# First K in three loads and four pieces, and job lists per PSUM bank in place of a list scheduler, in a fused attention and max-out kernel

## The chip, the cores and the metric

The kernel runs on one core of a Trainium2 chip. Its time is the device time of one execution in microseconds; lower is better. The core has a tensor engine (PE; its weight loads are listed as PEld), a vector engine (DVE), a scalar engine (ACT), GpSimd (POOL) and a sync engine (SP) whose queue issues nearly all DMAs. Sixteen DMA engines move the data.

## The reference

Queries are pooled by pairs of rows, attention is computed for 8 batches of 8 heads, and the result goes through a max-out layer:

```python
q_pool = q.reshape(B, H, S // 2, 2, D).mean(axis=3)      # B, H = 8, 8; S = 1152; D = 64
scores = np.matmul(q_pool, k.transpose(0, 1, 3, 2)) / np.sqrt(D)
attn = softmax(scores)                                    # over the keys
x = np.matmul(attn, v).transpose(0, 2, 1, 3).reshape(B * S // 2, H * D)
out = np.maximum(x @ w1, x @ w2) @ w_out                  # 4608 x 512, inner width 1024
```

All inputs and the output are float32. A guarded slow path (functions `guarded`, `softmax_head`, `softmax_rows`, `maxout`) is taken only where a sum of exponentials leaves a safe range; with these inputs it is not taken.

## The kernel before

**Tiling.** Two heads make a pair; there are 32 pairs. For each pair the kernel loads q, k and v (576 KB each), adds the two query rows of a pooling pair (`cast_q0` on DVE for the first two pairs, `cast_q` on POOL for the others), casts k to bf16 into `kbf` and transposes it into `kT` (nine tiles of 128 keys, called columns here; the first five pairs on PE with a DVE copy out of PSUM, `ktrans_pe`, the others by a transposing DMA). `scores(g)` then makes the scores of 512 (query, key) columns of both heads in a PSUM tile `sps`, and ACT takes their exponential into `et` (L745). Three such tiles are used in turn until group 33, two behind it. A pair is 10 1/8 groups. In pair 0 the queries come in two runs, so that groups 0 to 3 and half of group 4 need only the first 256 queries: group 0 needs key columns 0 and 1, group 1 columns 2 and 3, group 2 columns 4 and 5, group 3 columns 6 and 7.

**Behind the exponentials.** PE multiplies `et` with v (`av_jobs`, L649 and L661), DVE normalizes into `xnat`, which is transposed into `xT`. The max-out is computed as relu(x (w1 - w2)) w_out + x (w2 w_out): `wd` is w1 - w2 (POOL), `w21` is w2 times w_out (PE, L870), the hidden block is L925 or, for two PSUM banks at once, L952, and the output L985 or L1018. The weights are loaded between the first pairs' tensors and are cast by DVE reductions (L823, L827).

**The start.** The first K comes in two loads, columns 0-4 and 4-9, with the two halves of the first Q around them. ACT casts columns 0-2 and 2-4 (L519), POOL columns 4-9 (L522); PE transposes the three pieces and DVE copies them into `kT` (L625). Until real work is there PE runs groups of dummy matmuls on a constant tile (`fill`, L464, four of 128 columns; `short`, L473, eight of 64), which write a PSUM bank that nobody reads.

**What sets the order.** A `Plan` holds operations with the names that they read and write and derives the semaphore waits. `Plan.op` also keeps a model of the time of every engine. In the program's last part a list scheduler (`refill`, `options`, `choose`, `steady`, with a table of tuning values by time) uses that model to pick which job's next unit goes to PE. A job is a list of PE units and an evacuation; each of the eight PSUM banks ("0" to "7" in the strings) holds one job at a time. After that `Plan.reorder` puts the operations of PE, DVE, POOL and SP into the order of four written strings, in which a letter or digit names a lane (bank, load kind, "S" for a score group) and the dummy groups are letters of their own (U, V, y, z, Y, Z). ACT has no string: its order is that of creation.

**The names and lines that are spoken of.** `load_k` L484, `load_q` L494, `cast_k0` L519 and L522, `cast_k` L510, `cast_q0` L536, `cast_q` L543, `qtrans0` L585 and L592, `ktrans_pe` L618 and L625, `scores` L738 and L745, `w2t_job` L841 and L847, `h_jobs` relu on ACT L932, `p_job` copy on ACT L1045 and its last piece L1030 and L1034, `store` L889.

Of the kernel before, what the change touches and what calls it, by code (L numbers as in the profile page):

```python
# [9 lines left out]
P = 128  # L10
# [9 lines left out]
class Plan:  # L20

    INORDER = ("PE", "ACT", "DVE", "POOL")
    LAT = {"PE": 0.182, "ACT": 0.181, "DVE": 0.010, "POOL": 0.010}
    HEAR = {"PE": 0.046, "ACT": 0.024, "DVE": 0.024, "POOL": 0.075, "SP": 0.05}

    def __init__(self):
        self.ops = []
        self.writer = {}
        self.readers = {}
        self.free = {}  # L30
        self.dma_free = 0.0
        self.mode = None
        self.act_end = 0.0
        self.last = {}

    def deps(self, r, w, after=()):
        raw = {self.writer[k] for k in r if k in self.writer}
# [5 lines left out]
        return deps, raw  # L43

    def when(self, eng, r=(), w=(), after=(), fence=False):

        if any(k not in self.writer for k in r):
            return 1e9
        t = self.free.get(eng, 0.0)
        for d in self.deps(r, w, after)[0]:  # L50
            p = self.ops[d]
            if p["eng"] != eng or p["dma"] is not None or fence:
                t = max(t, p["seen"] + self.HEAR[eng])
        return t

    def op(self, eng, fn, r=(), w=(), dma=None, cost=0.1, mode="f", after=(), solo=False,
           fence=False):
        n = len(self.ops)
        assert all(k in self.writer for k in r), r
        deps, raw = self.deps(r, w, after)  # L60
        prev = self.last.get(eng)
        if prev is not None and (solo or self.ops[prev]["solo"]):
            deps.add(prev)
            raw.add(prev)
        self.last[eng] = n
        t = self.when(eng, r, w, after, fence)
        if dma is not None:
            if not self.dma_free:
                t = 0.78
            self.free[eng] = t + (1.3 if mode == "t" else 0.5)  # L70
            a = max(self.free[eng] + 1.2, self.dma_free)
            self.dma_free = a + cost + (0.9 if a < 5.0 <= a + cost else 0.0)
            seen = self.dma_free + 0.5
        else:
            if eng == "PE" and mode != self.mode:
                t = max(t, self.free.get("PE", 0.0) + 0.098)
                self.mode = mode
            busy = cost
            seen = t + cost + self.LAT[eng]
            if eng == "ACT":  # L80
                busy = cost + 0.051
                seen = max(seen, self.act_end + cost + 0.0735)
                self.act_end = seen
            elif eng == "DVE":
                busy = cost + 0.012
            self.free[eng] = t + busy
        self.ops.append(dict(eng=eng, fn=fn, deps=deps, raw=raw, dma=dma, w=tuple(w),
                             seen=seen, end=self.free[eng], solo=solo, fence=fence, r=tuple(r), at=n))
# [7 lines left out]
    def lane(self, o):  # L96
        key = (o["w"] or ("o",))[0]
        if o["eng"] == "PE":
            return "S" if key[0] == "s" else key[1:]
# [9 lines left out]
    def reorder(self, want):  # L109
# [5 lines left out]
        for eng, text in want.items():  # L115
            lanes = {}
            for n in line[eng]:
                lanes.setdefault(self.lane(ops[n]), []).append(n)
            assert sorted(c for c in text if c not in self.fill) == sorted(
                c for c, v in lanes.items() for _ in v)  # L120
            line[eng] = []
            for c in text:
                if c in self.fill:
                    m, mode, fn = self.fill[c]
                    key = f"f{m}"
                    nxt = ops[lanes[str(m)][0]]
                    n = len(ops)
                    ops.append(dict(
                        nxt, fn=fn, w=(key,), r=(), raw={self.writer["warm"]}, fence=False, at=n, inc=False, mode=mode, cost=0.0,
                        deps={d for d in nxt["deps"] if key in ops[d]["w"] and ops[d]["eng"] != eng}  # L130
                        | {self.writer["warm"]}))
                    nxt["deps"].add(n)
                    line[eng].append(n)
                else:
                    line[eng].append(lanes[c].pop(0))
# [75 lines left out]
class Job:  # L211


    def __init__(self, kind, units, evac, done=None, nb=None, single=None):
        self.kind, self.units, self.evac, self.done = kind, units, evac, done
        self.nb = nb
        self.single = single
# [137 lines left out]
def bass_funnel_attn__then__act_maxout2_kernel(  # L355
# [38 lines left out]
    with outer:  # L394
# [50 lines left out]
        def setup():  # L445
# [11 lines left out]
            op("DVE", lambda e: e.memset(xnat[0][:, 0, 0, :], 1.0), w=["warm"], cost=0.0)  # L457

        def fill(m, mode):
            z = slice(0, P) if mode == "f" else rows(0)  # L460
# [6 lines left out]
            return m, mode, go  # L467
# [85 lines left out]
        def unit(r, cost, go, mode="f"):  # L553

            def plan_it(m):
                op("PE", lambda e: go(e, m), r=r, w=[f"f{m}"], cost=cost, mode=mode)
# [1107 lines left out]
```

## Time and profile before

| what | us |
|---|---|
| median of 3 runs (364.25 to 365.19) | 365.12 |
| span of the profiled execution, first to last instruction | 363.3 |
| PE busy | 354.4 |
| ACT busy | 314.7 |
| DVE busy | 242.1 |
| POOL busy | 124.4 |

The profiled execution is listed by its span; the runs' time holds what lies around it as well. PE's busy time counts dummy matmuls, and matmuls are pipelined, so busy does not mean at peak. A group that ends the idle time of another engine is named behind an arrow. A DMA's time runs from its issue to its landing, queueing included.

### The profile page before, as it was taken

Reading aid. Unit: us, or ns where it says so; the run is one execution under the profiler, and the core shown is the slowest. Engines: PE = TensorE matmul, PEld = TensorE weight load, DVE = VectorE, ACT = ScalarE, POOL = GpSimd, SP = SyncE. Lnnn points to the kernel's source line nnn. Section 1 sums busy time; section 2 is a strip of 40 time slices with the busy share of each in tenths; the row PEclk is TensorE's granted clock in tenths of the full one; section 3 lists DMA queues with packets and bytes.
Section 4 is the critical chain, followed back from the end, with each engine's and each line's share of the span. In section 5 each row is a group of like instructions: output and inputs, shape, how many; then the busy total and the mean of one; then the engine's idle time right before and its main releaser. Section 6 shows DMA issues by size and latency. Waiting matters only on the chain.

```text
span 363.3 us, 13384 instructions
## 1 busy us (share of the span) xinstructions
PE 354.4 (98%) x5973; PEld 222.3 (61%) x5973; DVE 242.1 (67%) x526; ACT 314.7 (87%) x355; POOL 124.4 (34%) x111
## 2 busy tenths in 40 slices
PE   7998999999999999999999999999999999999995
PEld 6675655666564666657575665666666566656842
DVE  2777468877589777948968595676977847715421
ACT  4999999989999999999999999999999989894221
POOL 1246986344045433452251604613424320010000
PEclk9999999999999999999999999999999999999999
DMA  7999999999859998996999999986999570723106
GB/s 261 403 395 396 403 278 325 233 311 308 212 98 265 280 291 248 232 267 152 315 297 210 239 298 299 294 258 161 249 252 241 162 163 12 190 47 68 41 6 174
DMA packets 77790, 84.78 MB, mean 233 GB/s; under 512 B 50080, under 2 KB 50848, under 8 KB 77728
## 3 DMA queue, kind: packets, MB, share of 16 engines
q1 hardware_dynamic: 77168, 83.09, 85.8%
q8 instruction: 48, 0.79, 0.9%
q10 hardware_dynamic: 560, 0.79, 0.7%
q14 instruction: 14, 0.11, 0.1%
HBM read 62.91 MB, written 9.44 MB: 199 GB/s over the span
## 4 chain that ended last, share of the span: by engine, by line
PE 89%; ACT 7%; DMA 1%; issue 0%; SPq 0%; POOL 0%; DVE 0%; DVEq 0%
PE sps L738 20%; PE sps L649 13%; PE sps L985 11%; PE fb L985 10%; PE sps L952 9%; ACT et L745 7%; PE fb L649 7%; PE fb L952 7%; PE sps L1018 3%; PE sps L661 2%; PE fb L870 2%; PE fb L1018 1%; PE sps L925 1%; DMA kraw<-in_k_dram 1%; PE fb L661 1%; PE fb L925 1%
## 5 line engine op out<-in xcount | busy, mean ns | idle before, releaser
L745 ACT ACTIVATE et<-sps 128x1024 bf16<-128x1024 f32 (+1 forms) x336 | 306.7, 1006 | 19.7 <-PE sps L738 17.8
L738 PE MATMUL sps<-qpT,kT 64*128 64x256 bf16 (+7 forms) x1162 | 118.4, 283 | 0.7 <-ACT et L745 0.3
L603 DVE STREAM_TRANSPOSE qpT<-qp 32x288 bf16<-32x288 bf16 x216 | 101.4, 469 | 5.6 <-PE sps L738 1.5
L738 PEld LDWEIGHTS sps<-qpT,kT 64*128 64x128 bf16 x1162 | 47.9, 94 | 48.4 <-ACT et L745 16.3
L543 POOL TENSOR_TENSOR qp<-qraw 128x576 bf16<-128x576 f32 x30 | 42.1, 1405 | 89.6 <-DVE qpT L603 66.0
L549 POOL TENSOR_SCALAR vE<-vraw 128x1152 bf16<-128x1152 f32 x32 | 36.8, 1151 | 65.8 <-DMA vraw<-in_v_dram 63.4
L649 PE MATMUL sps<-vE,et 128*128 128x65 bf16 x1368 | 48.6, 193 | 0.4 <-issue 0.4
L649 PEld LDWEIGHTS sps<-vE,et 128*128 128x128 bf16 x1368 | 43.7, 97 | 6.5 <-issue 5.6
L510 POOL TENSOR_SCALAR kbf<-kraw 128x1152 bf16<-128x1152 f32 x31 | 35.6, 1151 | 33.4 <-DMA kT<-kbf 16.8
L952 PE MATMUL sps<-xT,wd 64*128 64x512 bf16 (+3 forms) x368 | 43.4, 326 | 0.0
L985 PE MATMUL sps<-wo,stage 64*128 64x512 bf16 x256 | 36.8, 376 | 0.0
L952 PE MATMUL fb<-xT,wd 64*128 64x512 bf16 (+3 forms) x272 | 33.5, 333 | 0.1
L649 PE MATMUL fb<-vE,et 128*128 128x65 bf16 x936 | 33.1, 193 | 0.0
L985 PE MATMUL fb<-wo,stage 64*128 64x512 bf16 x224 | 33.0, 376 | 0.0
L649 PEld LDWEIGHTS fb<-vE,et 128*128 128x128 bf16 x936 | 29.8, 97 | 4.8 <-issue 4.1
L961 DVE TENSOR_SCALAR stage<-sps 128x1024 bf16<-128x1024 f32 (+3 forms) x23 | 22.3, 969 | 15.4 <-PE sps L952 15.2
L961 DVE TENSOR_SCALAR stage<-fb 128x1024 bf16<-128x1024 f32 (+3 forms) x17 | 17.0, 999 | 10.7 <-PE fb L952 10.4
L952 PEld LDWEIGHTS sps<-xT,wd 64*128 64x128 bf16 x368 | 15.6, 94 | 13.5 <-PE sps L952 1.4
L671 DVE RECIPROCAL rcs<-sps 128x5 f32<-128x5 f32 (+1 forms) x38 | 7.0, 185 | 20.0 <-PE sps L649 19.5
L985 PE MATMUL sps<-w,xT 64*128 64x512 bf16 x128 | 18.8, 376 | 0.0
L996 DVE COPY stage<-sps 128x1024 f32<-128x1024 f32 x8 | 9.8, 1225 | 12.8 <-PE sps L985 12.7
L985 PEld LDWEIGHTS sps<-wo,stage 64*128 64x128 bf16 x256 | 12.1, 94 | 9.5
(88 smaller groups left out, 292.9 us busy)
## 6 DMA issues: line engine op xcount, KB each, us to landing
vraw<-in_v_dram SPq DMA_DIRECT2D x32, 576.0 KB, 6.6
kraw<-in_k_dram SPq DMA_DIRECT2D x31, 576.0 KB, 6.3
qraw<-in_q_dram SPq DMA_DIRECT2D x31, 576.0 KB, 6.1
out_dram<-stage SPq DMA_DIRECT2D x21, 256.0 KB, 5.8
out_dram<-stage SPq DMA_DIRECT2D x23, 128.0 KB, 3.3
xT<-in_moe_w_dram SPq DMA_DIRECT2D x4, 512.0 KB, 10.3
stage<-in_moe_w_out_dram SPq DMA_DIRECT2D x4, 512.0 KB, 14.0
stage<-in_moe_w_dram SPq DMA_DIRECT2D x4, 512.0 KB, 13.7
```

Of the source, the lines that this page charges most:

```text
L510: op("POOL", lambda g: g.tensor_scalar(kbf[s][:, :, :, :].rearrange("p t h d -> p h t d"), kraw[r][:, :, :, :], 1.0, 1.0, ALU.mult, ALU.mu ...
L543: op("POOL", lambda g: g.tensor_tensor(qpf[s][:, :, :], qraw[r][:, :, 0, :], qraw[r][:, :, 1, :], ALU.add), r=[f"qraw{r}"], w=[f"qp{s}.0", ...
L549: op("POOL", lambda g: g.tensor_scalar(vE[r][:, :, :, 0:D].rearrange("p t h d -> p h t d"), vraw[r][:, :, :, :], 1.0, 1.0, ALU.mult, ALU.m ...
L603: op("DVE", lambda e: e.transpose(view[dst:dst + 32, :, 32 * pb:32 * pb + 32], qpf[s][src:src + 32, :, 32 * db:32 * db + 32]), r=[f"qp{s}. ...
L649: last = e.matmul(fb[m][:, sb * 66:sb * 66 + 65], et[:, a:a + P], vE[vs][:, t, half, 0:65], start=(t == 0), stop=(t == NT - 1))
L661: last = e.matmul(fb[m][rows(half), NCH * 66:NCH * 66 + 65], et[:, a:a + NB], vE[vs][:, t, half, 0:65], start=(t == 0), stop=(t == NT - 1))
L738: last = e.matmul(sps[r][:, h, col:col + hi - lo], kT[i % 3][rows(h), t, :], qpT[i % 3][rows(h), lo:hi], start=True, stop=True)
L745: op("ACT", lambda e: e.activation(et2[:, :, c:c + z - a], sps[r][:, :, a - g * W:z - g * W], EXP, scale=scale), r=[f"s{r}"], w=keys + ([f ...
L952: last = e.matmul(fb[m + k][:, 0:size], wd[z, ct, (f0 + k) * P:(f0 + k + 1) * P], xT[z, ct, n0:n1], start=(turn == 0 and ct == 0), stop=(t ...
L961: dve(lambda e: e.tensor_scalar_max(gT[:, f0:f0 + 2, g0:g0 + size], wide[m // 2][:, :, 0:size], 0.0), [f"f{m}", f"f{m + 1}"], w + [f"f{m}" ...
L985: last = e.matmul(fb[m + k][:, :], lhs, rhs, start=(turn == 0 and j == 0), stop=(turn == 1 and j == NC_ + NF - 1))
L1018: return e.matmul(fb[m][:, 0:c1 - c0], lhs, rhs[:, c0:c1], start=(j == 0), stop=(j == NC_ + NF - 1))
```

## The change

There are two parts.

The loads and the pieces of the first K: three loads (columns 0-2, 2-6, 6-9), each with a semaphore of its own, and four pieces (0-2, 2-4, 4-6 on ACT, 6-9 on POOL), each cast, transposed by PE and copied by DVE. The first line of the PE string, the DVE string and the SP string change with it; the first score group goes alone ahead of the transposes of columns 2-6, and three groups of four dummy matmuls stand where five stood.

The schedule: the model of time, the scheduler and its tables go. In their place stands a list of jobs for each bank; one loop walks the PE string and creates each unit, each evacuation and, as soon as what they need has been created, the loads, casts and transposes. So PE's operations are created in their final order (the dummies too), while DVE, POOL and SP are still put into the order of their strings. ACT's order follows from the new order of creation.

```diff
-        K0 = (0, 2, 4, NT)
+        K0 = (0, 2, 4, 6, NT)
+        K0_LOADS = (0, 2, 6, NT)
...
-                    w=["kraw0.0"] if hi < NT else [f"kraw{s}"],
-                    dma="d_k" if hi < NT else f"d_k{s}", cost=0.0 if lo else 1.54)
+                    w=[f"kraw0.{lo}"] if hi < NT else [f"kraw{s}"],
+                    dma=f"d_k.{lo}" if hi < NT else f"d_k{s}")
...
             if hi < NT:
-                op("ACT", lambda e: e.activation(dst, src, COPY), r=["kraw0.0"], w=[f"kbf0.{lo}"],
-                   cost=(hi - lo) * 2 * D / 1200.0 + 0.03)
+                op("ACT", lambda e: e.activation(dst, src, COPY), r=[f"kraw0.{max(x for x in K0_LOADS if x <= lo)}"],
+                   w=[f"kbf0.{lo}"])
...
+        jobs_of = {
+            "0": "q0.0 k0.2 k0.6 q0.4 w1 q1.0 k1.5 w2 a0.1 k2.5 x0 a1.0 q3 k3.5 W0 W2 a4.0 H0.6 a6.0 "
...
+            "1": "k0.0 k0.4 k1.0 a0.0 q2 k2.0 w0 a1.1 w3 k3.0 x1 a4.1 a6.1 a8.1 a9.1 a10.1 a16.1 a17.1 "
...
         pe_order = (
-            "VVVVVVU0zz01SS0zzzSS0YSSYYSYYYS01SY0Sz0SSYSYY1S101S110SS000S1S01S01SSS000001S1S11SSS10SS101SS0S0"
+            "VVVVVVU01yS01SS0zzS0YSSYYSYYYS01SY0Sz0SSYSYY1S101S110SS000S1S01S01SSS000001S1S11SSS10SS101SS0S0"
...
+            later("lk0", [], lambda: load_k(0, tuple(zip(K0_LOADS, K0_LOADS[1:]))))
+            later("lq0", [], lambda: load_q(0, ((0, Q0[1]), (Q0[1], QU))))
+            later("cq0", ["lq0"], lambda: (cast_q0(0, 0, Q0[1]), cast_q0(0, Q0[1], QU)))
+            later("ck0", ["lk0"], lambda: [cast_k0(lo, hi) for lo, hi in zip(K0, K0[1:])])
...
+        for c in pe_order:
+            if c == "S":
+                scores(nxt)
+                nxt += 1
...
+            elif c in fills:
+                m, fn = fills[c]
+                op("PE", fn, r=["warm"], w=[f"f{m}"])
+            else:
+                m = int(c)
+                if c not in lane:
+                    name = left[c].pop(0)
+                    lane[c] = name, make(name)
+                name, job = lane[c]
+                job.units.pop(0)(m)
+                if not job.units:
...
+                    def end(c=c, m=m, job=job):
+                        job.evac(m)
+                        del lane[c]
...
+            settle()
...
         dve_order = (
-            "QQ0010Q0WQ0100WW0W1111001010W1W000W11010101W666666767TTT6T07T667T666TTTTTT60TTTTT006100T1T6TTTT6"
+            "QQ01010Q0WQ0100WW0W1111001010W1W000W11010101W666666767TTT6T07T667T666TTTTTT60TTTTT006100T1T6TTTT6"
...
         sp_order = (
-            "qkkqkwqvwwwqkwvwwwqkwwkvvqqqkwwvqtkqkvtkqktvkxxtvkqvtxxkxxqqkqqtvoxvxtvooxvxqtqkvqtokxokotkkxoov"
+            "qkkkqkwqvwwwqkwvwwwqkwwkvvqqqkwwvqtkqkvtkqktvkxxtvkqvtxxkxxqqkqqtvoxvxtvooxvxqtqkvqtokxokotkkxoov"
...
-        plan.reorder({"PE": pe_order, "DVE": dve_order, "POOL": pool_order, "SP": sp_order})
+        plan.reorder({"DVE": dve_order, "POOL": pool_order, "SP": sp_order})
```

`settle` runs everything that waits in `later`'s list for names that have been made; `make` turns a name of the lists into a job (`q` and `k` transposes, `a` attention times v, `x` transposes of the result, `w` and `W` weights, `h` and `H` hidden blocks, `p` and `P` outputs).

More of the change, by code (lines that the diff above doesn't have):

```diff
@@ L42, in deps @@
             deps.update(self.readers.get(k, ()))
[L43 to L88, printed above, removed]
+        self.ops.append(dict(eng=eng, fn=fn, deps=deps, raw=raw, dma=dma, r=tuple(r), w=tuple(w),
+                             fence=fence, at=n))
         for k in r:
@@ L118, in reorder @@
                 lanes.setdefault(self.lane(ops[n]), []).append(n)
[L119 to L135, printed above, removed]
+            assert sorted(text) == sorted(c for c, v in lanes.items() for _ in v)
+            line[eng] = [lanes[c].pop(0) for c in text]
         place = {}
```

774 lines of the change are left out of this document (187 added, 587 removed), and 14 rows, old and new, of the table jobs_of.

## The prediction

> **What bounds the kernel now.** I read the stages first (busy time of each engine per stretch), then the chain that ended last, then the timeline of the first 16 us, then the two places where data from memory meets that chain. The stages:
>
> ```profile
> core 0: us, PE busy (x) PEld busy (x) DVE busy (x) ACT busy (x) POOL busy (x), PEclk, DMA share, GB/s
> 3.75:4.75 1.00, 0.98 (x20) 0.79 (x18) 0.43 (x1) 0.20 (x1) 0.00 (x0) 1.00 0.93 306
> 5.50:7.25 1.75, 0.75 (x11) 0.28 (x10) 0.47 (x2) 0.99 (x2) 0.73 (x1) 1.00 0.96 342
> 17.25:30.00 12.75, 12.58 (x278) 8.97 (x276) 10.38 (x21) 12.75 (x16) 6.58 (x6) 1.00 1.04 396
> 30.00:34.00 4.00, 3.14 (x54) 2.07 (x56) 2.80 (x7) 4.00 (x5) 2.19 (x2) 1.00 1.05 391
> 36.00:41.00 5.00, 5.00 (x89) 2.79 (x86) 0.92 (x2) 4.87 (x6) 5.00 (x5) 1.00 1.03 407
> 41.00:359.66 318.66, 317.71 (x5305) 196.58 (x5301) 218.29 (x480) 278.59 (x315) 105.98 (x88) 1.00 0.87 217
> ```
>
> From 36 us to the last evacuation at 359.66 the tensor engine is busy 322.71 of 323.66 us: there the kernel is as long as its matmuls, and their order and number stay. So a change of the start is worth only what it moves the tensor engine's arrival at about 36 us. Until then the stages show a second limit: the DMA share is 0.93 to 1.05 from 4 us on, so loads land when the bytes in front of them are through, not when they are asked for.
>
> The chain that ended last, in order of time, over the first 45 us:
>
> ```profile
> 1.73 4.63 DMA kraw<-in_k_dram
> ...
> 6.44 0.74 POOL kbf L522
> 7.18 0.05 issue
> 7.22 0.45 PE fb L618 x5
> 7.68 0.67 PE fb L464 x12
> 8.35 0.34 PE sps L738 x4
> 8.69 0.02 issue
> 8.71 26.76 ACT et L745 x30
> ```
>
> Read alone it says: the second part of the first K lands at 1.73 + 4.63 = 6.36, is cast in one piece of 0.74, transposed, and then thirty exponentials run without a gap from 8.71 to 35.47 (0.89 each). Whoever gets the third exponential out before 8.71 would then win that time. The ScalarE's own rows (timeline: start, duration, line, what it writes and reads, count, idle before and who ended it) show a hole ahead of the third:
>
> ```profile
> 4.54 0.72 ACT L519 ACTIVATE kbf<-kraw 128x256 bf16<-128x256 f32 x2 [2.47 <-DMA kraw<-in_k_dram]
> 6.26 1.94 ACT L745 ACTIVATE et<-sps 128x1024 bf16<-128x1024 f32 x2 [1.00 <-PE sps L738]
> 8.71 1.02 ACT L745 ACTIVATE et<-sps 128x1024 bf16<-128x1024 f32 x1 [0.51 <-PE sps L738]
> ```
>
> Two exponentials, then 0.51 of waiting for the third group's scores, whose kT comes from the second load.
>
> **The change part by part.** Its first part is the loads. The first K arrives as columns 0-2, 2-6 and 6-9 in place of 0-4 and 4-9.
>
> ```profile
> 1.27 0.93 SPq L484 DMA_DIRECT2D kraw<-in_k_dram  x2
> 2.24 0.47 SPq L494 DMA_DIRECT2D qraw<-in_q_dram  x1
> ```
>
> ```profile
> kraw<-in_k_dram SPq DMA_DIRECT2D x1, 320.0 KB, 4.6
> qraw<-in_q_dram SPq DMA_DIRECT2D x1, 320.0 KB, 5.1
> qraw<-in_q_dram SPq DMA_DIRECT2D x1, 256.0 KB, 3.0
> kraw<-in_k_dram SPq DMA_DIRECT2D x1, 256.0 KB, 3.3
> ```
>
> The sync queue issues one DMA more, 0.47, ahead of the second half of Q and of everything behind it in that queue (the next K, the first weights, Q of pair 1, the first V). The Q half is issued at 2.24 and lands 5.1 later, so a later issue of 0.47 is hidden by the transfers in front of it; without that cover it would cost 0.47. Bytes stay equal, packets rise from 512 to 768 (each is one row's columns). The price of 256 more packets is not in the trace. Upper end: packets of 1 to 1.3 KB move 306 GB/s (3.75 to 4.75), those of 2.3 KB and more 396 GB/s (17.25 to 30); as a fixed time for each packet that is 1152/306 - 1.79 x 1.152 = 1.7 ns, with the slope (2304/396 - 1152/306)/1.152 = 1.79 ns a KB, and 256 of them make 0.44 us. [...] I take 0.1, nearer to nothing, since 3.75 to 4.75 still belongs to the start-up and its rate is low for other reasons too. [...]
>
> Landings: part one has half the bytes of today's first, 131 KB at 306 GB/s = 0.43 earlier than 4.54, so 4.11 to 4.54. Part two ends two columns into today's second load, which needs 6.36 - 4.54 = 1.82 for five columns: pro rata 5.27; by the rate 4.54 + 0.43 = 4.97; at the latest with today's second load, 6.36.
>
> The casts: the ScalarE casts columns 0-2, 2-4 and now 4-6, all three ahead of its first exponential, since its order is that of creation. So here is an added wait: exponential 0 now stands behind a cast that needs load two. Two casts take 0.72, so exponential 0 starts at 5.27 + 0.72 + 0.06 = 6.05 (from 5.75 to 7.14), today 6.26. GpSimd casts three columns in place of five, 0.44 for 0.74, and the four transposed pieces need one more VectorE copy; both engines idle there (DVE 0.47 busy in the 1.75 us from 5.50), cost nothing. On the tensor engine three groups of four dummy matmuls stand where five stood, and the first score group runs alone ahead of columns 2-6. If nothing waits, the hole of 0.51 is gone: exponentials back to back from 6.05, where the present run, counted back from 8.71 at 0.89 each, begins in effect at 6.93. The start gains 0.9 us (from 1.2 down to a loss of 0.2).
>
> **How much of it arrives.** Two places ahead of 36 us are clocked by memory and not by the ScalarE. First, pair 1. VectorE, TensorE and ScalarE rows:
>
> ```profile
> 10.47 1.22 DVE L823 TENSOR_REDUCE xT<-xT 128x1024 bf16<-128x1024 f32 x1 [0.94 <-DMA xT<-in_moe_w_dram]
> 11.96 0.76 DVE L536 TENSOR_TENSOR qp<-qraw 128x576 bf16<-128x576 f32 x1 [0.27 <-DMA qraw<-in_q_dram]
> ```
>
> ```profile
> 14.73 0.40 PE L618 MATMUL fb<-ident,kbf 128*128 128x128 bf16 x4
> 15.06 0.46 PE L738 MATMUL sps<-qpT,kT 64*128 64x64 bf16 x6
> ```
>
> ```profile
> 15.96 1.11 ACT L745 ACTIVATE et<-sps 128x1024 bf16<-128x1024 f32 x1
> 5.83 0.61 PE L738 MATMUL sps<-qpT,kT 64*128 64x256 bf16 x8 [0.22 <-DVE kT L625]
> ```
>
> The w2 cast and pair 1's Q both wait for their DMA; from them follow, in the fixed order of the VectorE and the tensor engine, the w2 and Q copies, the second half of K1 (14.73) and score group 10 (15.06), with no ScalarE wait between. An exponential follows its scores' start by 6.26 - 5.83 = 0.43, so exponential 10, now at 15.96, cannot start before 15.49: of 0.9 at most 0.47 is left. Second, pair 3:
>
> ```profile
> 17.56 1.00 SPq L484 DMA_DIRECT2D kraw<-in_k_dram  x1
> kraw<-in_k_dram SPq DMA_DIRECT2D x1, 576.0 KB, 13.4
> 29.64 1.41 POOL L543 TENSOR_TENSOR qp<-qraw 128x576 bf16<-128x576 f32 x1 [0.34 <-DMA qraw<-in_q_dram]
> 31.16 1.15 POOL L510 TENSOR_SCALAR kbf<-kraw 128x1152 bf16<-128x1152 f32 x1
> 32.45 0.22 PE L618 MATMUL fb<-ident,kbf 128*128 128x128 bf16 x1 [0.21 <-DVE qpT L576]
> ```
>
> K of pair 3 lands at 17.56 + 13.4 = 30.96, whatever the ScalarE did, because the DMA engines are full (1.04). GpSimd ends its cast at 32.31 and the tensor engine transposes it at 32.45. The wait named there is VectorE's, which follows the shifted stream; right behind it stands GpSimd, which does not. So at most 32.45 - 32.31 less a semaphore's 0.04 = 0.10 of the gain gets past 32.45; the rest becomes idle time of the tensor engine in 30 to 34, where it idles 0.86 already. From there everything is tensor work. A loss, in contrast, is not clipped: the VectorE wait would move on.
>
> The schedule's second part, job lists for the scheduler, leaves the tensor engine's order behind its first line as it was, and the VectorE and SP strings gain one letter each. The ScalarE's order is not written out and now follows the creation order: near the end two pairs change places.
>
> ```profile
> 352.01 0.38 ACT L932 ACTIVATE stage<-sps 128x256 bf16<-128x256 f32 x1 [5.17 <-PE sps L925]
> 352.30 0.58 ACT L1045 COPY stage<-sps 128x512 f32<-128x512 f32 x1
> ```
>
> The output copy (352.30) goes ahead of the last hidden block's relu (352.01). The ScalarE idled 5.17 before that, so the copy and its store run in that gap; the relu waits for its matmuls as now. Gain nothing to 0.1, cost nothing; if the copy came late the relu would, by at most the copy's 0.58.
>
> Sum: 0.10 gained at 32.45, 0.10 lost to packets (K3 lands later too), up to 0.1 at the end: -0.05 us on the span of 363.3. The median of the runs shown, 365.12, is 1.8 above that span, the part outside it, which stays. Forecast 365.0 us.
>
> **The rivals.** B, the whole start arrives: if VectorE latencies and not GpSimd hold pair 3, and pair 1's chain slides as well, 0.9 to 1.2 us come through: 364.2 to 363.9. For it: the unbroken run of thirty exponentials. Against it: the rows at 10.47, 11.96 and 31.16. C, slower, one mechanism: exponential 0 behind the third cast. If load two lands like today's second, at 6.36, exponential 0 starts at 7.14, 0.21 behind the effective 6.93, the scores of groups 1 and 2 stand behind the same cast, and with the packets' 0.44 it is 365.8. It passes 0.3% from a landing at 6.8 on with the packets' full price, at 7.25 without it (8.03 less 0.78). For it: today's second load is the slowest of the four by its bytes (4.6 for 320 KB right behind 3.3 for 256 KB). D, slower: with fewer dummies the tensor clock drops. Row 5.50 shows 0.75 busy of 1.75 at a granted 1.00, so holes of that size do not do it; if they did, these 0.75 and as much again would double: 365.9 to 366.6. [...] E, the change does nothing to the start because columns 2-6 come no sooner: 365.1.
>
> **How the numbers follow.** A measurement of this kernel can tell about 0.3%, 1.1 us; the runs shown lie 0.94 apart. Forecast A with E 0.66, all same; B 0.18, of it 0.14 faster beyond 1.1 with the scatter and 0.04 within; C 0.12, of it 0.06 slower; D 0.04 slower. That makes 0.14 faster, 0.76 same, 0.10 slower. The likeliest case alone spans 364.6 to 365.5; the range takes in most of B and C, 364.0 to 365.9.
>
> **What would show it.** Right: three casts on the ScalarE, exponential 0 at about 6.05, no hole before the third; score group 10 still near 15; K3's cast still ending near 32.3 and its transposes within 0.1 of 32.45; more tensor idle time in 30 to 34 than 0.86. Wrong: K3's transposes at 31.9 or earlier (B), exponential 0 beyond 6.9 (C), a granted clock below 1.00 before 16 us (D), or any new idle time behind 36 us, which would mean that the lists changed more than the start.

## The result and the profile after

The changed kernel takes 366.17 us in the median of 22 runs (364.68 to 370.39); the kernel before, beside it on the same chip, 364.99 (364.03 to 366.18, 22 runs). The ratio is 1.0041, 95% interval 1.0025 to 1.0058: slower, with an interval that leaves out 1, and above the forecast's range (364.0 to 365.9). The median lies 1.2 us above the predicted 365.0.

The ratios leave out executions more than 1.5% above the fastest of their kernel (one here), but the change alters how often an execution takes some 4 us more, so those above 367.9 us are counted below for every kernel (5 of the 22 here, none of the 22 of before).

The profiled execution has a span of 364.5 us, before 363.3. Stages of the changed kernel, columns as in the prediction (line numbers from here on are those of the changed kernel: L450 and L441 cast K on the ScalarE and on GpSimd, L467 adds Q's rows, L542 transposes K, L661 makes the scores, L668 their exponential):

```profile
3.75:4.75 1.00, 1.00 (x21) 0.84 (x18) 0.27 (x2) 0.42 (x1) 0.00 (x0) 1.00 0.67 135
5.50:7.25 1.75, 1.00 (x11) 0.38 (x12) 0.43 (x2) 1.23 (x3) 0.51 (x1) 1.00 1.01 356
...
12.00:17.25 5.25, 4.54 (x81) 3.01 (x79) 4.00 (x7) 5.11 (x6) 1.15 (x1) 1.00 1.04 407
17.25:30.00 12.75, 12.15 (x263) 8.86 (x261) 10.46 (x21) 12.48 (x15) 6.37 (x6) 1.00 1.04 396
30.00:34.00 4.00, 3.84 (x73) 2.45 (x69) 3.07 (x7) 3.90 (x6) 2.41 (x2) 1.00 1.05 392
36.00:41.00 5.00, 4.69 (x59) 1.98 (x57) 1.52 (x3) 4.87 (x6) 5.00 (x5) 1.00 1.03 406
41.00:359.66 318.66, 318.23 (x5337) 197.49 (x5336) 218.00 (x479) 279.47 (x315) 106.37 (x88) 1.00 0.89 217
```

Two things differ. Between 3.75 and 4.75 us the DMA engines move 135 GB/s where they moved 306. And in 30 to 34 the tensor engine, which idled 0.86 there, idles 0.16: its stream comes later, so the slack in front of pair 3 is gone. In 36 to 41 it idles 0.31 (before 0.00), behind 41 us 0.43 (before 0.95), together 0.74 where it was 0.95. All of the loss of this execution is made at the start. The ScalarE's rows of the timeline there:

```profile
3.93 0.42 ACT L450 ACTIVATE kbf<-kraw 128x256 bf16<-128x256 f32 x1 [1.86 <-DMA kraw<-in_k_dram]
6.02 0.72 ACT L450 ACTIVATE kbf<-kraw 128x256 bf16<-128x256 f32 x2 [1.67 <-DMA kraw<-in_k_dram]
6.65 3.80 ACT L668 ACTIVATE et<-sps 128x1024 bf16<-128x1024 f32 x4
10.79 2.85 ACT L668 ACTIVATE et<-sps 128x1024 bf16<-128x1024 f32 x3 [0.34 <-PE sps L661]
```

Three casts, the first exponential at 6.65, four in a row, and then a new hole of 0.34 at 10.79. Where that hole and the rest come from, the loads by issue (KB, us from issue to landing; the sync queue issues Q's halves at 0.79 and 2.75, the three K parts at 1.27, 1.73 and 2.24, the next K at 3.26):

```profile
kraw<-in_k_dram SPq DMA_DIRECT2D x1, 576.0 KB, 7.0
qraw<-in_q_dram SPq DMA_DIRECT2D x1, 320.0 KB, 6.0
...
kraw<-in_k_dram SPq DMA_DIRECT2D x1, 256.0 KB, 4.3
kraw<-in_k_dram SPq DMA_DIRECT2D x1, 192.0 KB, 4.4
kraw<-in_k_dram SPq DMA_DIRECT2D x1, 128.0 KB, 2.6
```

Part two lands at 1.73 + 4.3 = 6.0, Q's second half at 2.75 + 6.0 = 8.8 where it was 2.24 + 5.1 = 7.3, and the next K at 10.2 to 10.3. That K's row of before, issued at 2.75, puts its landing at 9.2:

```profile
kraw<-in_k_dram SPq DMA_DIRECT2D x1, 576.0 KB, 6.4
```

So the loads behind the third part come over 1 us later in this trace, and what is clocked by them follows. The changed kernel's rows for pair 1 and pair 3:

```profile
13.04 0.76 DVE L467 TENSOR_TENSOR qp<-qraw 128x576 bf16<-128x576 f32 x1 [0.26 <-DMA qraw<-in_q_dram]
16.14 0.61 PE L661 MATMUL sps<-qpT,kT 64*128 64x64 bf16 x8
31.36 1.15 POOL L441 TENSOR_SCALAR kbf<-kraw 128x1152 bf16<-128x1152 f32 x1
33.41 0.68 PE L542 MATMUL fb<-ident,kbf 128*128 128x128 bf16 x9
```

Pair 1's Q is cast 1.08 later (before 11.96), score group 10 begins 1.08 later (before 15.06), the transposes of pair 3 0.96 later (before 32.45), and there they stand 0.90 behind GpSimd's cast (31.36 + 1.15), which no longer limits them; in the chain of before the transposes follow such a cast by 0.04 (7.18 to 7.22), the prediction's figure for a semaphore.

That was one execution. A second one of the same kernel, profiled in the experiments below (e13), shows the other part of the loss. Its span and clock, and its stages; the column behind the five engines is the granted clock:

```profile
core 0: 366.9 us, clock 0.985
```

```profile
3.75:4.75 1.00, 1.00 (x21) 0.78 (x18) 0.23 (x2) 0.42 (x1) 0.00 (x0) 1.00 0.85 218
5.50:7.25 1.75, 0.78 (x8) 0.23 (x4) 0.29 (x1) 1.09 (x3) 0.47 (x1) 1.00 0.88 288
7.25:12.00 4.75, 4.28 (x48) 2.89 (x49) 2.07 (x5) 3.65 (x5) 1.19 (x2) 0.56 1.02 369
12.00:17.25 5.25, 5.25 (x52) 4.39 (x51) 2.36 (x4) 3.67 (x4) 1.15 (x1) 0.50 1.04 406
```

From 7.81 to 18.05 us (10.24 us by the record of the clock) the tensor engine was granted half its clock. In 12 to 17.25 it is busy all the time and does 52 matmuls, where the first trace has 81 in 4.54 busy. The mean clock of a run does not always tell. The record of the clock begins with its first change, at 5.23 us in the first trace, and counts what lies in front of it as full; but there, too, the matmuls are slow: in the first trace eight matmuls that transpose Q take 0.42 us at 4.24 and ten take 0.34 at 9.36, and in e3, whose record begins at 9.92, the tensor engine is busy 3.41 us with 31 matmuls in the 3.41 us in front of that and 2.98 with 60 in as much time behind it. Two of the four runs of e13 above 367.9 us have a mean of 1.000, so no lost stretch is on their record. That their full clock first came late is likely, but no trace of such a run was kept.

### The profile page after: what moved, and what is told of

Read it like the earlier page. It is cut to its first block, busy times and chain, and to the rows that moved or that the text cites. A ratio compares the mean times of both kernels' runs of the same rounds, so it can differ in the third digit from the quotient of the medians.

```text
span 364.5 us, 13368 instructions
## 1 busy us (share of the span) xinstructions
PE 354.9 (97%) x5961; PEld 222.2 (61%) x5965; DVE 242.4 (67%) x527; ACT 315.7 (87%) x356; POOL 124.4 (34%) x111
## 4 chain that ended last, share of the span: by engine, by line
PE 93%; DMA 2%; ACT 2%; SPq 1%; DVE 0%; issue 0%; DVEq 0%
PE sps L661 21%; PE sps L572 12%; PE sps L893 11%; PE fb L893 10%; PE sps L860 9%; PE fb L572 8%; PE fb L860 7%; PE sps L923 3%; DMA qraw<-in_q_dram 2%; PE sps L584 2%; ACT et L668 2%; PE fb L785 2%; PE fb L584 2%; PE fb L923 1%; PE sps L833 1%; PE fb L833 1%
## 5 line engine op out<-in xcount | busy, mean ns | idle before, releaser
L668 ACT ACTIVATE et<-sps 128x1024 bf16<-128x1024 f32 (+1 forms) x336 | 307.2, 1003 | 18.9 <-PE sps L661 16.7
L661 PE MATMUL sps<-qpT,kT 64*128 64x256 bf16 (+7 forms) x1162 | 119.2, 283 | 0.4 <-ACT et L668 0.3
L661 PEld LDWEIGHTS sps<-qpT,kT 64*128 64x128 bf16 x1162 | 48.4, 94 | 48.1 <-ACT et L668 16.3
L441 POOL TENSOR_SCALAR kbf<-kraw 128x1152 bf16<-128x1152 f32 x31 | 35.6, 1150 | 37.2 <-DMA kT<-kbf 19.9
L893 PEld LDWEIGHTS sps<-wo,stage 64*128 64x128 bf16 x256 | 12.1, 94 | 9.5
```

The lines of the kernel that those rows point to most:

```text
L441: op("POOL", lambda g: g.tensor_scalar(kbf[s][:, :, :, :].rearrange("p t h d -> p h t d"), kraw[r][:, :, :, :], 1.0, 1.0, ALU.mult, ALU.mu ...
L661: last = e.matmul(sps[r][:, h, col:col + hi - lo], kT[i % 3][rows(h), t, :], qpT[i % 3][rows(h), lo:hi], start=True, stop=True)
L668: op("ACT", lambda e: e.activation(et2[:, :, c:c + z - a], sps[r][:, :, a - g * W:z - g * W], EXP, scale=scale), r=[f"s{r}"], w=keys + ([f ...
L893: last = e.matmul(fb[m + k][:, :], lhs, rhs, start=(turn == 0 and j == 0), stop=(turn == 1 and j == NC_ + NF - 1))
```

## The experiments

The theories were P (the three short loads let the DMA engines run low, so all loads behind them land later), W (the first exponential stands behind the third cast), L (the lists changed more than the start) and, from e5 on, H (with fewer dummies the tensor engine loses its clock; the forecast's rival D). Results first. "Above" counts executions above 367.9 us; "rest" is the mean of the others less the mean of such runs of the kernel before on the same chip; the kernel before has 6 of 155 above. "Dummy groups" counts those of the first 10 us that the change reduced from five to three.

| run | loads of the first K | dummy groups | above | rest, us | ratio, 95% interval |
|---|---|---|---|---|---|
| the change | 0-2, 2-6, 6-9 | 3 | 5 of 22 | +0.86 | 1.0041 (1.0025 to 1.0058) |
| e5, the change again | same | 3 | 4 of 12 | +0.45 | 1.0043 (1.0016 to 1.0069) |
| e13, the change again | same | 3 | 4 of 12 | +1.21 | 1.0050 (1.0020 to 1.0081) |
| e12, part three behind Q | same | 3 | 5 of 12 | +0.81 | 1.0061 (1.0030 to 1.0092) |
| e11 and e14 | same | 5 | 0 of 12, 0 of 12 | +0.17, +0.68 | 1.0012 (0.9996 to 1.0029), 1.0018 (0.9994 to 1.0041) |
| e3, old pieces | same | 5 | 0 of 12 | +0.31 | 1.0002 (0.9978 to 1.0026) |
| e6 | same | 8 | 2 of 11 | +1.54 | 1.0061 (1.0036 to 1.0085) |
| e4 and e15 | 0-6, 6-9 | 3 | 2 of 12, 0 of 12 | -0.03, +0.13 | 0.9993 (0.9958 to 1.0028), 0.9999 (0.9977 to 1.0020) |
| e16 | 0-6, 6-9 | 5 | 0 of 12 | +0.93 | 1.0020 (0.9999 to 1.0040) |
| e1, lists alone | 0-4, 4-9 | 5 | 1 of 12 | -0.06 | 1.0006 (0.9976 to 1.0036) |
| e2, new pieces | 0-4, 4-9 | 3 | 3 of 12 | +0.33 | 1.0019 (0.9984 to 1.0055) |
| e10 | 0-4, 4-9 | 3 | 5 of 12 | +0.37 | 1.0047 (1.0016 to 1.0079) |
| e7 | 0-4, 4-9 | 0 | 6 of 6 | none | 1.0101 (1.0077 to 1.0126) |
| e8 | 0-4, 4-9 | 8 | 1 of 12 | +1.56 | 1.0044 (1.0026 to 1.0062) |
| e9, a load more | 0-4, 4-9 | 5 | 0 of 12 | +1.14 | 1.0030 (1.0013 to 1.0046) |

**One part at a time.** e1 is the change with the old loads, pieces and strings, so the lists alone ("..." stands for lines left out, here of the lists and the other strings):

```diff
-        K0 = (0, 2, 4, 6, NT)
-        K0_LOADS = (0, 2, 6, NT)
+        K0 = (0, 2, 4, NT)
+        K0_LOADS = (0, 4, NT)
...
-            "VVVVVVU01yS01SS0zzS0YSSYYSYYYS01SY0Sz0SSYSYY1S101S110SS000S1S01S01SSS000001S1S11SSS10SS101SS0S0"
+            "VVVVVVU0zz01SS0zzzSS0YSSYYSYYYS01SY0Sz0SSYSYY1S101S110SS000S1S01S01SSS000001S1S11SSS10SS101SS0S0"
...
```

> The job lists alone: loads, pieces and first lines of the orders as in the kernel before. Theory P (the start-up loads run dry: the three K loads bring 256 packets more, and all that is queued behind them lands about 1.1 us later): within 0.1% of the kernel before, K of pair 1 lands near 9.2 as before. Theory W (exponential 0 waits behind the third cast on the ScalarE): the same, 365.0. Theory L (the lists change the work after 41 us): about 366, with new idle time of the tensor engine behind 41 us.

365.25 us in the median, ratio 1.0006: L is out. e2 keeps the old two loads and takes the four pieces with their order; the third piece, whose columns span both loads, is cast by GpSimd:

```diff
-        K0_LOADS = (0, 2, 6, NT)
+        K0_LOADS = (0, 4, NT)
...
-            if hi < NT:
+            if hi <= 4:
                 op("ACT", lambda e: e.activation(dst, src, COPY), r=[f"kraw0.{max(x for x in K0_LOADS if x <= lo)}"],
...
```

> Job lists and the four pieces with their orders, but the two loads of before (columns 0-4 and 4-9); columns 4-6 are cast by GpSimd and not by the ScalarE, so that no exponential stands behind them. Theory P: no delay of the loads, so within 0.1% of the kernel before; by the clip of the prediction the hole of 0.51 ahead of the third exponential goes and the total still moves by less than 0.2 us. If the start passed to the end instead: 0.3 to 0.5 us faster. Theory L: about 366.

365.83, ratio 1.0019, which is not clear of noise; but 3 of 12 runs are above 367.9 us, and its trace had half the clock from 7.18 to 10.60 us, with the loads of before. That speaks for H and for nothing in P. e3 takes the three loads and leaves the pieces and the order old:

```diff
-        K0 = (0, 2, 4, 6, NT)
+        K0 = (0, 2, 4, NT)
...
-                   r=["kraw0"], w=[f"kbf0.{lo}"])
+                   r=["kraw0.2", "kraw0"], w=[f"kbf0.{lo}"])
...
-            "VVVVVVU01yS01SS0zzS0YSSYYSYYYS01SY0Sz0SSYSYY1S101S110SS000S1S01S01SSS000001S1S11SSS10SS101SS0S0"
+            "VVVVVVU0zz01SS0zzzSS0YSSYYSYYYS01SY0Sz0SSYSYY1S101S110SS000S1S01S01SSS000001S1S11SSS10SS101SS0S0"
...
```

> Job lists and the three loads (columns 0-2, 2-6, 6-9), but the three pieces, the casts and the orders of before. Theory P: slower as the change is, 0.2% to 0.5%, K of pair 1 lands near 10.2 in place of 9.2, and the DMA engines move under 200 GB/s between 3.5 and 4.75 us. Theory W: within 0.1% of the kernel before, since only two casts stand ahead of exponential 0.

365.72, ratio 1.0002. Its stage and the next K's load (issued at 3.26):

```profile
3.75:4.75 1.00, 1.00 (x21) 0.87 (x19) 0.26 (x2) 0.42 (x1) 0.00 (x0) 1.00 0.53 90
```

```profile
kraw<-in_k_dram SPq DMA_DIRECT2D x1, 576.0 KB, 5.7
```

The dip is there, deeper, and yet the next K lands at 9.0, earlier than before. So the dip by itself is not the lateness, a miss for P as I had put it. The span of this trace is 1.2 us above before all the same (364.5); here the full clock came only at 9.92 us. e4 loads columns 0-6 and 6-9 and keeps the rest of the change:

```diff
-        K0_LOADS = (0, 2, 6, NT)
+        K0_LOADS = (0, 6, NT)
...
-            "qkkkqkwqvwwwqkwvwwwqkwwkvvqqqkwwvqtkqkvtkqktvkxxtvkqvtxxkxxqqkqqtvoxvxtvooxvxqtqkvqtokxokotkkxoov"
+            "qkkqkwqvwwwqkwvwwwqkwwkvvqqqkwwvqtkqkvtkqktvkxxtvkqvtxxkxxqqkqqtvoxvxtvooxvxqtqkvqtokxokotkkxoov"
```

> The change with two loads, columns 0-6 and 6-9, and its four pieces and orders. Theory P: 512 packets as before, K of pair 1 lands near 9.2, no stretch under 250 GB/s behind 3 us; exponential 0 only at about 7.2, since its columns land near 5.2, so 0.2 to 0.4 us slower than before. Theory W (the wait and not the loads makes the loss): slower than the change itself, 366.2 or more.

365.46, ratio 0.9993: without the third load the loss is gone from the median, though 2 of 12 runs are above 367.9 us. The first exponential starts at 6.69, as in the changed kernel, so W is out too.

**Dummies and clock.** e5 is the change once more. e6 has five groups of dummies more than the change, e7 the old loads and the lists without the five groups, e8 the same with three more, eight in all (its expectation miscounts them as six). The edits of e7 and e8 are shown against e1:

In e6:

```diff
-            "VVVVVVU01yS01SS0zzS0YSSYYSYYYS01SY0Sz0SSYSYY1S101S110SS000S1S01S01SSS000001S1S11SSS10SS101SS0S0"
+            "VVVVVVU01ySzzz01SS0zzSzz0YSSYYSYYYS01SY0Sz0SSYSYY1S101S110SS000S1S01S01SSS000001S1S11SSS10SS101SS0S0"
```

In e7:

```diff
-            "VVVVVVU0zz01SS0zzzSS0YSSYYSYYYS01SY0Sz0SSYSYY1S101S110SS000S1S01S01SSS000001S1S11SSS10SS101SS0S0"
+            "VVVVVVU001SS0SS0YSSYYSYYYS01SY0Sz0SSYSYY1S101S110SS000S1S01S01SSS000001S1S11SSS10SS101SS0S0"
```

In e8:

```diff
-            "VVVVVVU0zz01SS0zzzSS0YSSYYSYYYS01SY0Sz0SSYSYY1S101S110SS000S1S01S01SSS000001S1S11SSS10SS101SS0S0"
+            "VVVVVVU0zz01SSzzz0zzzSS0YSSYYSYYYS01SY0Sz0SSYSYY1S101S110SS000S1S01S01SSS000001S1S11SSS10SS101SS0S0"
```

> The changed kernel itself, run again, for a second trace and a second comparison. Theory P (the three short loads let the DMA engines run low at 3.3 to 5 us, and every load behind them lands about 1.1 us later): the dip to about 100 to 150 GB/s between 3.75 and 4.75 us is there again, the second K lands near 10.2 us (before 9.16), w2's first part near 11.5 (before 10.45), and the kernel is slower by .3 to .5%. Theory H (what counts is whether TensorE keeps its full clock before 12 us, and that differs from run to run): the landings can be as late as they like, the time goes by the clock record of the trace; ratio 1.002 to 1.006, and a profile whose full clock comes by 5.3 us and stays would be within .3 us of before. Theory W (the first exp waits for the third cast): exp of the first scores at 6.6 to 6.7 us, a loss of .4 us and no more.

> The changed kernel with five groups of dummy matmuls more in the first 12 us (three behind the third score group, two behind the sixth). H: TensorE has less idle time there, the full clock comes as early as before the change and stays; the time falls back to that of the kernel before (ratio .999 to 1.001). P: the loads land as late as in the changed kernel (second K near 10.2 us) and the dummies change nothing: ratio 1.003 to 1.005. W: nothing, 1.003 to 1.005; were the dummies in the way of real work instead, .2 to .5 us more than that.

> The kernel with the change's lists but the old loads and pieces, without the five groups of dummies of the other bank in the first 12 us. Its loads are those of before. H: the full clock comes late or is lost for a time before 12 us; slower by .3 to 1.3 us (ratio 1.001 to 1.0035). P: with the old loads the second K lands near 9.2 us and nothing is lost: ratio .9995 to 1.0005. W: the same as P.

> The same lists, old loads and pieces, with six groups of dummies more instead. H: the full clock is there by 5 us in every execution; faster by 0 to .4 us (ratio .999 to 1.000), with fewer executions above 366 us than the kernel before has. P and W: ratio .9995 to 1.0005; where a dummy group stands in front of a score group that is ready, up to .3 us slower.

e5 repeats the loss (365.76, 4 of 12 above) with the next K at 9.77, half as late as in the first trace. e7 takes 369.03, all six executions above, with the loads of before: far beyond what I gave H. Its stages:

```profile
5.50:7.25 1.75, 0.62 (x9) 0.23 (x8) 0.33 (x2) 1.16 (x2) 0.01 (x1) 1.00 0.91 318
7.25:12.00 4.75, 2.97 (x34) 2.00 (x35) 2.08 (x4) 2.72 (x3) 1.87 (x2) 0.54 1.03 407
12.00:17.25 5.25, 5.25 (x52) 4.38 (x49) 1.63 (x4) 3.88 (x4) 1.16 (x1) 0.50 1.04 403
```

The same half clock from 7.63 to 17.87 us, in an execution with a mean clock of 0.984; the other five have 1.000. But e6 (367.19, 2 of 11 above) and e8 (366.9, 1 of 12) missed: more dummies did not give the time back. The rest of their runs lie 1.5 us above before, e8's with loads that are the old ones. Why is not shown. That dummies stand in front of real work cannot be all of it: in e8's trace the exponential that starts at 50.38 us in before starts 0.34 later, the one at 72.71 1.48 later and the one at 264.90 2.23 later, far behind the dummies. The chain there has idle stretches of 0.28 us at 66.11 and 0.42 at 73.13 with nothing waited for that the profile shows, and a wait for a transposing DMA that lands at 265.45.

**Each cause apart.** e9 is e1 with one load of 384 KB that nobody reads, in front of Q's second half. e10 is e1 with three groups of dummies. e11 is the change with five. e12 is the change with the third K part issued behind Q's second half. The edits of e9 and e10 are shown against e1, those of e11 and e12 against the change:

In e9:

```diff
+            if i == 0:
+                op("SP", lambda e: e.dma_start(
+                    vraw[2][:, :, 0:6, :].rearrange("p h t d -> p h (t d)"), v[b, 2:4, :, :].rearrange("h (p t) d -> p h (t d)", t=NT)[:, :, 0:6 * D]),
+                    w=["kspare", "vraw2"], dma="d_spare")
```

In e10:

```diff
-            "VVVVVVU0zz01SS0zzzSS0YSSYYSYYYS01SY0Sz0SSYSYY1S101S110SS000S1S01S01SSS000001S1S11SSS10SS101SS0S0"
+            "VVVVVVU0z01SS0zzSS0YSSYYSYYYS01SY0Sz0SSYSYY1S101S110SS000S1S01S01SSS000001S1S11SSS10SS101SS0S0"
```

In e11:

```diff
-            "VVVVVVU01yS01SS0zzS0YSSYYSYYYS01SY0Sz0SSYSYY1S101S110SS000S1S01S01SSS000001S1S11SSS10SS101SS0S0"
+            "VVVVVVU01ySz01SS0zzzS0YSSYYSYYYS01SY0Sz0SSYSYY1S101S110SS000S1S01S01SSS000001S1S11SSS10SS101SS0S0"
```

In e12:

```diff
-            "qkkkqkwqvwwwqkwvwwwqkwwkvvqqqkwwvqtkqkvtkqktvkxxtvkqvtxxkxxqqkqqtvoxvxtvooxvxqtqkvqtokxokotkkxoov"
+            "qkkqkkwqvwwwqkwvwwwqkwwkvvqqqkwwvqtkqkvtkqktvkxxtvkqvtxxkxxqqkqqtvoxvxtvooxvxqtqkvqtokxokotkkxoov"
```

> The change's lists with the old two loads of the first K, the old three pieces and the old dummies, and one load more of 393 KB, which nobody reads, between the first K and the second half of the first Q. Nothing but the landings of what stands behind it moves: by 393 KB at about 390 GB/s, some 1.0 us, as the three-part load did in the changed kernel's trace (+1.08 for the second K). Theory P (the late landings alone are the loss): slower by .3 to 1.0 us, ratio 1.001 to 1.003, with the shift against the kernel before growing between 8 and 25 us. The forecast's clip read the other way, or theory H (only the clock counts): ratio .9995 to 1.0005.

> The change's lists, old loads and pieces, with three groups of dummies of the other bank instead of five, which is the changed kernel's number. Theory H (with fewer dummies more executions lose the full clock between 7 and 11 us): 2 or more of its 12 runs above 368 us, where the kernel before has 4 of 84; median up by .3 to 1 us. P: nothing, ratio .9995 to 1.0005 and no more runs above 368 us than before has.

> The changed kernel with five groups of dummies of the other bank instead of three, as many as before. H: the runs above 368 us go (none or one of 12, where the changed kernel has 10 of 34), and the rest stays .3 to .5 us above the kernel before, for the loads. P: as the changed kernel, 1.003 to 1.005. If dummies stand in the way of real work, as in the two kernels with more of them: 1.004 to 1.006 with no run above 368 us.

> The changed kernel with the third part of the first K issued behind the second half of the first Q instead of in front of it. P in the form that three short loads in a row let the engines run low: the larger load of Q fills the gap, the dip of 3.75 to 4.75 us goes or is halved, the second K lands by 9.4 us, and the time is within .2 us of before; the third part itself lands .7 us later, for at most .2 us. P in the form that the number of loads or of packets counts: the second K lands near 10 us all the same, ratio 1.003 to 1.005. H: nothing moves but the clock; as the changed kernel.

(The changed kernel had 9, not 10, of 34 above by then, the kernel before 4 of 85.) e9: 366.33, ratio 1.0030, none above: late loads alone cost. In its trace pair 1's Q lands at 13.37 us (before 11.94) and its transposes start at 15.13 (before 13.70). The half clock from 15.49 to 18.90 us in that trace comes on top, so the 1.4 us in the median are not the landings alone. But the two hang together there: the tensor engine's wait of 1.17 us for the late Q lies in the 3.41 us behind which the clock was lost. e10: 366.03, ratio 1.0047, 5 of 12 above: three groups alone bring the lost clock, on the old loads. Its stages:

```profile
7.25:12.00 4.75, 4.22 (x46) 3.19 (x47) 2.55 (x5) 2.79 (x4) 1.20 (x2) 0.50 1.03 407
12.00:17.25 5.25, 5.25 (x52) 4.39 (x51) 1.62 (x3) 3.68 (x4) 1.15 (x1) 0.50 1.04 406
```

e11: 365.22, ratio 1.0012, none above. Its trace keeps the clock, and has the dip too:

```profile
3.75:4.75 1.00, 1.00 (x21) 0.84 (x18) 0.32 (x2) 0.42 (x1) 0.00 (x0) 1.00 0.63 134
5.50:7.25 1.75, 1.50 (x16) 0.81 (x16) 0.44 (x2) 1.41 (x3) 0.47 (x1) 1.00 1.00 368
7.25:12.00 4.75, 4.33 (x79) 3.34 (x77) 2.21 (x5) 4.63 (x6) 1.20 (x2) 1.00 1.03 386
```

e12: 366.62, ratio 1.0061, 5 of 12 above; the dip stays (108 GB/s in 3.75 to 4.75), the next K lands at 9.67. So the place of the third part in the order is not what makes the loads behind it late.

**Two by two on one chip.** Three loads or two (0-6, 6-9), three groups or five: e13 is the change, e14 is e11's kernel, e15 e4's, and e16 has both edits.

> The changed kernel (three loads, three groups of dummies) on the chip of the next three runs, so that its two suspected causes are taken away one at a time and together on one chip. So far 24 of 82 runs of kernels with three groups came out above 367.9 us, and 5 of 168 with the five groups of before in their places. Theory P and H added: 3 to 4 of 12 above 367.9 us, the others .4 to .9 us above the kernel before; ratio 1.003 to 1.006. H alone: the others within .2 us of before. P alone: no more above 367.9 us than before has.

> The changed kernel with five groups of dummies: the lost clock taken away, the three loads kept. P and H added: none or one of 12 above 367.9 us, and .3 to .8 us above before, ratio 1.001 to 1.002. H alone: within .2 us of before. P alone: as the changed kernel, 1.003 to 1.006.

> The changed kernel with its first K in two loads of 384 and 192 KB instead of three: the short loads taken away, the three groups of dummies kept. P and H added: 3 to 4 of 12 above 367.9 us and the others within .2 us of before, second K landed by 9.3 us. H alone: the same. P alone: none above 367.9 us more than before has, within .2 us of before.

> Both taken away: two loads of 384 and 192 KB, five groups of dummies, the rest of the change kept. P and H added: nothing of the loss is left, ratio .998 to 1.0005, none or one of 12 above 367.9 us; with the second K landed near 8.6 us instead of 9.2 and the loads behind it as much earlier, up to .5 us faster than before. H alone: as with three loads and five groups. P alone: as with the same loads and three groups. A third cause in the pieces or the lists: still 1.001 or more.

With three loads, three groups 366.57 and five 365.41; with two loads, three groups 364.89 and five 365.72 (before 364.95). The two causes do not add up. Taking away the third load alone takes away the loss, most of the long executions included (2 of 24 above in e4 and e15, 18 of 58 with three loads and three groups). Putting the dummies back alone takes away the long executions (0 of 24) and leaves 0.2 to 0.7; the trace of e14 still lost the clock for 3.41 us, from 7.23. Doing both is no better than the second alone, a miss for the sum. What differs with two loads, e15's first stages and the ScalarE's rows show:

```profile
3.75:4.75 1.00, 0.81 (x19) 0.68 (x16) 0.42 (x1) 0.00 (x0) 0.00 (x0) 1.00 1.12 374
5.50:7.25 1.75, 1.26 (x16) 0.71 (x18) 0.67 (x3) 1.21 (x4) 0.51 (x1) 1.00 0.91 298
```

```profile
5.08 1.03 ACT L450 ACTIVATE kbf<-kraw 128x256 bf16<-128x256 f32 x3 [3.01 <-DMA kraw<-in_k_dram]
6.66 6.60 ACT L668 ACTIVATE et<-sps 128x1024 bf16<-128x1024 f32 x7 [0.55 <-PE sps L661]
```

All three casts end at 6.1, seven exponentials run without a hole, and the tensor engine is busy 1.26 of the 1.75 us from 5.50 (0.78 in e13). Whether that is why two loads need no more dummies is not shown: it is one trace, with the full clock from 4.97 us on. No kernel here is faster than the one before; e15 is level with it.

**The account.** Over the 46 runs of the changed kernel the mean is 1.67 us above the kernel before. 13 of them are above 367.9 us, 4.1 us over before's other runs: 13/46 x 4.1 = 1.2. The other 33 are 0.84 over: 33/46 x 0.84 = 0.6. Before's own long runs (6 of 155, about 0.15) come off. So some two thirds are the executions above 367.9 us, which go with the dummies and are rare with the loads 0-6 and 6-9. Eight of the 13 have a mean clock of 0.984 to 0.986, as the three traces with 10.24 us at half clock have (0.984 to 0.985); the other five have 0.999 or 1.000, and for them the late clock is argued, not shown. The last third goes with the third load (0.17 to 1.21 in the seven comparisons of kernels that have it and no more than five groups; -0.06 to 0.37 in e1, e2, e4, e10 and e15, which have not, though 0.93 in e16); three of the 33 runs have a mean clock of 0.993 to 0.995, as the traces with one lost stretch of 3.41 us have, and make 0.15 of the 0.6. How the remainder divides between late landings and a full clock that first came late was not told apart run by run.

## Why the prediction was wrong

- **Fewer dummies at no price, and rival D at 0.04.** This step failed, and most of the loss is here: the sum has no term for two groups of dummies less. The argument was that the stretch from 5.50 to 7.25 has 0.75 busy of 1.75 us at a granted 1.00, "so holes of that size do not do it". One execution was read as if it were all of them. e13 has 0.78 busy in the same stretch, hardly more, and loses the clock behind it; the kernel before itself comes out above 367.9 us 6 times in 155. With three groups it is 18 of 58 on three loads and 8 of 24 on the loads of before; with five groups 0 of 36 and 7 of 167. Rival D's mechanism was right; its size was not. The spans are 363.3 before, 364.0 to 365.7 in the traces that lost the clock for 3.41 us from 7 to 8 us on (e2, e12, e14, e16), and 366.9 to 367.6 in those that lost it for 10.24 us (e7, e10, e13): some 4 us and not D's 0.8 to 1.5, in 13 of 46 executions. That the median, 366.17, lies in D's 365.9 to 366.6 is luck: it stands between the many that lose little and the few that lose 4 us. Nor did it take an idle engine to lose the clock: in the 3.42 us at whose end e13 lost its clock, the first row under what stays open, the tensor engine was busy 2.22.
- **Packets, taken at 0.1, with 0.44 as the upper end.** Undersized, as far as the landings tell. The next K lands at 9.28 us in the mean of six traces with the loads 0-4 and 4-9 (8.96 to 9.56), at 9.64 in seven with three in the change's order (8.95 to 10.24): 0.36, near the end of the range that I had set aside as start-up. The two groups overlap, and the later issue of the next K (3.26, before 2.75) is in the 0.36 as well as the packets; no run parts the two. The first trace's 1.08 is the latest of the seven.
- **"A later issue of 0.47 is hidden by the transfers in front of it."** Wrong in part. Q's second half landed 1.5 later in the first trace (8.79, before 7.30), with the DMA engines at 0.67 in front of it. In the other six traces with three loads in this order it landed between 7.26 and 8.53, and in e3, with the engines at 0.53, at 7.46; so the holes in the cover alone do not give the delay.
- **Landings and casts.** Three casts, right. Part two at 5.81 to 6.31 in the traces with three loads in the change's order, not 5.27 (within the range given). The first exponential at 6.65, then, not 6.05: of the gain of 0.9 at the start 0.3 was left, and 0.34 of hole came back at 10.79. The hole ahead of the third exponential did go.
- **The clips.** "A loss, in contrast, is not clipped" held at the start: score group 10 at 16.14, pair 3's transposes 0.96 late, idle time in 30 to 34 down to 0.16, and e9's ratio for late loads alone. But further on part of it was taken up: in the first trace the exponential that starts at 43.75 in before starts 1.53 late and the one at 50.38 0.96 late, where the tensor engine's idle 0.39 of before in 45 to 52 us is gone. The sign named for it, more idle time in 30 to 34 than 0.86, failed with the gain that it was meant to catch.
- **Lists, ACT's order at the end, and no new idle behind 36 us.** Right: e1 is 1.0006, the idle time behind 36 us is 0.74 in all where it was 0.95 (0.31 of it is new, in 36 to 41), and the shift of the tensor engine's stream in the changed trace is constant at 1.1 us from 137 us to the end.
- **Rival C** (365.8 by the third cast and the packets) came near the measured time for the wrong reason: e4 has the same first exponential as the change, and no loss in the median. What was said for it misread the loads: by its bytes Q's second half, 5.1 us for 320 KB, is slower than K's second load, 4.6 for as much.

What stays open: why an execution with the same stretch of idle time loses the clock or keeps it. The 3.41 us between the first full clock and its loss in e13 and e14, and the same stretch in e1, which kept it:

```profile
4.39:7.81 3.42, 2.22 (x30) 1.00 (x28) 1.09 (x4) 1.65 (x4) 0.51 (x1) 1.00 0.97 302
```

```profile
3.82:7.23 3.41, 2.43 (x36) 1.33 (x33) 0.96 (x4) 1.45 (x4) 0.42 (x1) 1.00 0.91 279
```

```profile
4.49:7.90 3.41, 2.20 (x39) 1.54 (x34) 0.88 (x4) 2.43 (x4) 0.73 (x1) 1.00 1.01 321
```

No busy share divides them: 2.43 lost, 2.20 kept. But only near there do both occur. Measured in steps of 3.41 us (the time to the loss in seven traces) from the first full clock to 16 us, the six with 1.45 to 2.13 us busy (e7, e12, e2, e9, e10, e16) all lost it, and those with 2.45 to 3.22 all kept it. The lost ones begin between 3.8 and 4.6 us (and one of e9 at 12.1). Open, too, is why five groups cost 0.8 us against three on two loads (e16, e15). The trace of e16 lost the clock from 7.18 to 10.60 us and that of e15 did not, but the other runs of e16 show no such loss in their mean clock (0.999 or 1.000).

## What to carry to other kernels

Dummy matmuls are a setting to be measured, with many executions and their spread: too few lost the clock now and then here (18 of 58 executions above 367.9 us with three groups on three loads, none of 36 with five), which one profile does not show, and too many cost time as well (1.5 us with eight groups, for a reason that is not shown). Splitting an early load can cost the loads behind it: here the first cast began at 3.93 us where it had begun at 4.54, and the next K landed at 9.64 in the mean where it had landed at 9.28. This start is clocked by landings further on, and in the first trace the 1.08 by which the next K and pair 1's Q were late passed on almost whole (0.96 at pair 3's transposes); that a gain need not pass is the forecast's estimate. Before a hole is called harmless because the clock stood beside it, look at several executions.

## What the runs showed that I had not expected

Between the first full clock and the end of the work, half clock came in stretches of 3.41 or 10.24 us and never of another length, and began 3.41 us after the full clock had come in seven traces (e2, e7, e10, e12, e13, e14, e16). It came back after one stretch where the tensor engine was busy 3.18 to 3.41 us in it, and after three where it was busy 2.16 to 2.99 us in the first. The full clock first came between 3.77 (e2) and 9.92 us (e3). A late one seems to cost as well: e4 and e15 are one kernel on two chips, and with the full clock from 8.88 us the span is 364.7, from 4.97 us 363.6, though the next K lands earlier in the first (8.55 against 9.03). One kernel's executions differ in it: it first came at 5.23, 5.45 and 4.39 us in three traces of the changed kernel (the first one, e5 and e13).

Between 3.75 and 4.75 us the kernels with loads of 128, 256 and 192 KB moved 90 to 218 GB/s, those with 256 and 320 KB 170 to 306, those with 384 and 192 KB 351 to 384.
